# Sliding-window attention and two MLPs on one core: value products in quarter-array tiles, first query loads on ScalarE's queue, a new plan

## The chip, the cores and the metric

One NeuronCore of a Trainium2 chip runs the whole program. The metric is device time in microseconds, the median of several executions. Engines are named as in the profile: PE (TensorE, matmul), DVE (VectorE), ACT (ScalarE), POOL (GpSimd) and SP (SyncE, which issues DMAs).

## The reference

What is computed, cut to what matters:

```python
batch, n_heads, seq, head_dim = (2, 8, 768, 64)
n_sink, window = (4, 128)
scores = q @ k.T / sqrt(64); keep = is_sink | (0 <= row - col < window)
a = softmax(where(keep, scores, -1e9)); attn = a @ v
x = attn as (1536, 512)                  # tokens x model width
x = elu(x @ w_in) @ w_out                # 512 -> 2048 -> 512
x = (h - tanh(h)) @ w2_out, h = x @ w2_in
```

## The kernel before, in words

**Attention.** The 2 x 768 queries are 12 chunks `c` of 128 (six per batch). Each chunk has two groups `g` of four heads. A query needs the keys of its own chunk, of the one before (window 128) and the first eight keys (the sinks). `scores(g)` multiplies 64x64 tiles of the PE array, four at a time: the head width of 64 fills half the rows, and 64 queries fill half the columns. Each query half then has 128 keys in one "wide" piece, and a "thin" piece of 64 keys with 8 sink columns (72 columns). DVE adds the mask and takes the row's extreme in one instruction (a custom reduction, in the profile CUSTOM_DVE_ANT_0), ACT takes the exponential with its row sum, `norm(g)` divides, and `turn(g)` transposes the weights on PE into a PSUM bank, from which DVE or ACT copies them: `aT` (wide pieces), `aH` (thin pieces) and `aS` (sinks, split into a high and a low part).

**Value products.** `PV(c)` adds, for each of four head pairs, the sinks' product (all 128 columns), the wide pieces and the thin pieces into one bank of PSUM. The thin piece of a query half uses only 64 of the 128 key rows that stand in `aH`: the other 64 rows of its value tiles (`near_t`, `far_t`) are zeros, written once by eight memsets in `clear_values`, so each thin product streams through all 128 rows of the array, in a tile of 128x64 (two at once). Then `hi` and `lo` parts of the result are stored in `xhi` and `xlo`, the activations of the first MLP.

**MLPs.** Products are made in three float32r terms (high x high, high x low, low x high). `mlp_in` and `mlp_out` run over six phases of weight chunks; the first phase takes 256 tokens at a time (18 steps) and starts once two chunks of attention are done, all others take 512. Weights arrive as 64-bit words; `narrow` makes float32 of them (ACT, a clamp by `tensor_scalar`, then three DVE instructions), and `w_split` makes the two parts.

**What sets the order.** `Plan` records every instruction first, with the data it needs. `schedule` then simulates the engines with costs (`cost`), latencies between engines (`LAT`), a price for a change of the PE array's tiles (`SWITCH`), due times by kind of step (`DUE`), and the engines allowed for a kind (`PICK`), and fixes the order and the engine of every instruction. Where PE has nothing ready before the first `mlp_out`, it puts in idle matmuls (`idle`, a constant times a constant into bank 7), which keep PE busy: they are fixed instructions, executed whether or not the wait that they fill exists on the chip. All recorded instructions are issued from the line 404 (`emit` and the helpers), those of `many` (attention products) from line 165, idle matmuls from line 602.

The two lines that the change of the value products is about, for a thin piece (`last`):

```python
lhsT=part[:, kk, e, :] if last else whole[:, 2 * kk + e, :],
rhs=u[:, cols] if last else t[:, e, cols],
```

Of the kernel before, what the change touches and what calls it, by code (L numbers as in the profile page):

```python
# [7 lines left out]
F32 = mybir.dt.float32  # L8
# [8 lines left out]
P = 128  # L17
# [24 lines left out]
class Plan:  # L42
# [3 lines left out]
    ENGINES = ("PE", "ACT", "DVE", "POOL", "DMA")  # L46

    LAT = {
        "PE": {"PE": 0.0, "ACT": 205.0, "DVE": 210.0, "POOL": 235.0, "DMA": 200.0},
        "ACT": {"PE": 240.0, "ACT": 153.0, "DVE": 145.0, "POOL": 165.0, "DMA": 160.0},  # L50
        "DVE": {"PE": 262.0, "ACT": 130.0, "DVE": 127.0, "POOL": 160.0, "DMA": 130.0},
        "POOL": {"PE": 205.0, "ACT": 80.0, "DVE": 85.0, "POOL": 127.0, "DMA": 110.0},
        "DMA": {"PE": 2000.0, "ACT": 2000.0, "DVE": 2000.0, "POOL": 2000.0, "DMA": 0.0},
    }
# [3 lines left out]
    SWITCH = (95.0, 107.0, 55.0)  # L58
    BONUS, MARGIN = 159.46, 534669.58

    HOLD = {}
    DUE = {
        "c": (-4158.63, 122.021), "score": (-1557.88, 42.427), "norm": (-1579.49, 36.340), "end": (2474.55, 1.919),
# [7 lines left out]
        ("late w", "tensor_scalar", 512, False): ("DVE",), ("w", "tensor_scalar", 512, False): ("DVE",),  # L71
        ("T", "copy", 512, True): ("ACT",), ("norm", "tensor_scalar", 200, False): ("DVE",),
        ("late w", "copy", 512, False): ("ACT",), ("z", "copy", 512, False): ("ACT", "DVE"),
        ("ew", "tensor_tensor", 256, False): ("POOL",), ("late w", "tensor_tensor", 512, False): ("DVE",),
        ("late ew", "copy", 512, False): ("POOL",), ("out", "copy", 512, True): ("DVE",),
        ("late out", "copy", 512, True): ("DVE",), ("c", "tensor_copy", 128, False): ("POOL",),
        ("w", "copy", 512, False): ("ACT", "POOL"),
    }

    def __init__(self, tc):  # L80
# [7 lines left out]
        self.D = Rec(self, "DMA", nc.sync)  # L88

    def region(self, ap):  # L90
# [3 lines left out]
        if key not in self.masks:  # L94
            pstep, pn = dims[0]
            p0, e0 = divmod(off, pstep)
            psum = ap.space == PSUM
            grain = 512 if psum else (8 if pstep > 1024 else 1)
# [17 lines left out]
    def matmul_cost(kw):  # L116
# [5 lines left out]
        if kw["lhsT"].dtype == F32R:  # L122
            return n * 0.4233 + 10.3

        rows, cols = kw["lhsT"].shape[0] <= 64, kw["out"].shape[0] <= 64
        return (n / 1.2 + 2.5) * (0.5 if rows and cols else 1.0 if rows or cols else 2.0)

    @classmethod
    def cost(cls, eng, method, out, ins, kw):
# [6 lines left out]
        if eng == "ACT":  # L136
            t = (50.0 if psum else 100.0) + 0.833 * n
            return t + (94.0 if any(not isinstance(kw.get(k, 0.0), float) for k in ("scale", "bias")) else 0.0) \
                + (93.0 if "accum_out" in kw else 0.0) + (35.0 if "func" in kw else 0.0)
        if eng == "POOL":  # L140
            if method == "memset":
                return 60.0 + 0.5 * n
            return (60.0 + 3.6 * n if method == "tensor_scalar" else
                    60.0 + 1.8 * n if method == "tensor_copy" else 160.0 + 2.1 * n)
        if method in ("tensor_copy", "tensor_scalar", "memset") and not psum:
            return 75.0 + 0.525 * n
# [29 lines left out]
    def either(self, *recs, **kw):  # L176
# [7 lines left out]
        key = (self.tag[0], recs[1][1], cols, psum)  # L184
# [6 lines left out]
    def record(self, ways, args, kw, any_=False):  # L191
# [8 lines left out]
        for e, method, real in ways:  # L200
            if e == "DMA":
# [1042 lines left out]
```

## Time and profile before

| what | us |
|---|---|
| median of 3 runs (lowest, highest) | 626.07 (625.54, 627.9) |
| the profiled execution, its time | 626.38 |
| its span, first to last instruction | 624.6 |
| PE busy | 614.6 |
| DVE, ACT, POOL busy | 427.3, 239.8, 177.0 |

A busy PE is a PE whose instructions follow each other without a gap; their ends are modelled. What a piece of work costs PE is therefore read from start to start in the timeline, not from a row's mean. PE records a float32 product of attention as two matmuls, so 32 products are 64 records.

### The profile page before, as it was taken

To read this page: it belongs to the slowest core of one execution; us is meant where nothing else is said; L and a number is where in the kernel's file an instruction comes from. 1 tells how busy PE (TensorE), PEld (TensorE's weight loads), DVE (VectorE), ACT (ScalarE), POOL (GpSimd) and SP (SyncE) were. 2 spreads that over 40 slices of the span, in tenths; PEclk is the share of its full clock that TensorE was granted. 3 is DMA by queue.
4 is the path that set the end of the run, shared out by engine and by line. 5 is a ranking of instruction groups with operands and counts; after the bars stand their busy time and mean duration, and the time that the engine had idled before them with its cause. 6 is when DMAs were issued, how large, how long until landed. Compare 5 with 4: busy or idle time off the path is not lost.

```text
span 624.6 us, 11065 instructions
## 1 busy us (share of the span) xinstructions
PE 614.6 (98%) x4246; PEld 516.4 (83%) x4246; DVE 427.3 (68%) x955; ACT 239.8 (38%) x562; POOL 177.0 (28%) x225
## 2 busy tenths in 40 slices
PE   9999999999999999999999999999999999999995
PEld 6788889989888888888888888888888888888884
DVE  8889999999974779935379996368953543342232
ACT  6776978665413345332335441123411211111010
POOL 4335332403432333412121553223332121220120
PEclk9999999999999999999999999999999999999999
DMA  7577463443240122320012324022300000000012
GB/s 230 164 217 193 114 180 112 145 168 123 82 134 1 43 93 73 132 67 1 1 55 80 102 89 147 1 67 68 101 1 1 0 2 0 1 35 34 0 70 72
DMA packets 39038, 49.96 MB, mean 80 GB/s; under 512 B 25408, under 2 KB 26432, under 8 KB 38976
## 3 DMA queue, kind: packets, MB, share of 16 engines
q1 hardware_dynamic: 38976, 49.17, 25.1%
q8 instruction: 35, 0.57, 0.4%
q14 instruction: 27, 0.22, 0.1%
HBM read 46.01 MB, written 3.15 MB: 79 GB/s over the span
## 4 chain that ended last, share of the span: by engine, by line
PE 87%; DVE 6%; DMA 3%; ACT 2%; issue 1%; ACTq 0%; DVEq 0%
PE bank L404 78%; PE bank L165 8%; DVE arena L404 3%; DMA raw<-in_moe_w_in_dram 2%; DVE t L404 2%; PE bank L602 2%; ACT arena L404 1%; DVE w L404 1%; DMA arena<-in_kq_dram 1%; DMA small<-in_params_dram 0%; ACT t L404 0%; DVE xlo L404 0%; DVE xhi L404 0%; ACT arena_r L404 0%; DVE sm_all L404 0%
## 5 line engine op out<-in xcount | busy, mean ns | idle before, releaser
L404 PE MATMUL bank<-xhi,w 128*128 128x512 f32 (+1 forms) x840 | 246.5, 373 | 0.1
L404 POOL CAST arena_r<-arena 128x512 fp32r<-128x512 f32 (+2 forms) x115 | 80.2, 698 | 394.2 <-PE bank L404 234.4
L404 PEld LDWEIGHTS bank<-xhi,w 128*128 128x128 f32 x840 | 154.1, 188 | 27.8 <-DVE xhi L404 0.3
L404 PE MATMUL bank<-arena_r,w 128*128 128x512 f32 (+1 forms) x684 | 157.9, 358 | 0.7 <-DVE arena L404 0.6
L404 PE MATMUL bank<-w,arena_r 128*128 128x512 f32 (+1 forms) x594 | 154.3, 383 | 0.0
L404 PE MATMUL bank<-xlo,w 128*128 128x512 f32 (+1 forms) x420 | 143.8, 372 | 0.3 <-DVE xlo L404 0.3
L404 ACT ACTIVATE arena<-bank 128x512 f32<-128x512 f32 (+1 forms) x105 | 58.7, 559 | 221.5 <-PE bank L404 213.5
L404 PEld LDWEIGHTS bank<-arena_r,w 128*128 128x128 f32 x684 | 116.1, 189 | 20.5 <-DVE arena L404 1.6
L404 PEld LDWEIGHTS bank<-w,arena_r 128*128 128x128 f32 x594 | 109.4, 188 | 22.2
L404 DVE TENSOR_TENSOR arena_r<-arena,arena_r 128x512 fp32r<-128x512 f32 (+1 forms) x50 | 33.6, 673 | 85.4 <-PE bank L404 59.0
L404 PEld LDWEIGHTS bank<-xlo,w 128*128 128x128 f32 x420 | 78.9, 188 | 14.3 <-DVE xlo L404 0.5
L404 POOL TENSOR_TENSOR arena_r<-arena,arena_r 128x512 fp32r<-128x512 f32 (+3 forms) x77 | 79.1, 1029 | 25.8 <-ACT arena_r L404 6.9
L404 DVE TENSOR_TENSOR arena<-bank,arena 128x512 f32<-128x512 f32 (+1 forms) x65 | 43.1, 678 | 45.0 <-ACT arena L404 42.3
L404 ACT ACTIVATE arena<-arena 128x512 f32<-128x512 f32 (+1 forms) x73 | 42.3, 587 | 8.7 <-DVE w L404 6.1
L404 ACT ACTIVATE arena<-arena,nm_all 128x200 f32<-128x200 f32 (+1 forms) x96 | 42.2, 443 | 8.1 <-DVE nm_all L404 8.0
L165 PE MATMUL bank<-arena 128*64 128x64 f32 (+3 forms) x1376 | 43.5, 241 | 0.0
L165 PEld LDWEIGHTS bank<-arena 64*64 64x64 f32 (+1 forms) x1376 | 38.4, 135 | 4.8 <-issue 1.6
L404 DVE SCALAR_TENSOR_TENSOR arena<-arena,bank 128x512 f32<-128x512 f32 (+1 forms) x57 | 33.7, 595 | 12.6 <-ACT arena L404 12.6
L404 DVE TENSOR_SCALAR t<-t 128x512 f32<-128x512 f32 (+1 forms) x70 | 38.7, 559 | 1.6 <-ACT t L404 1.3
L404 DVE SCALAR_TENSOR_TENSOR t<-raw,t 128x512 uint32<-128x512 uint32 x54 | 39.7, 738 | 0.2
L404 DVE TENSOR_TENSOR w<-arena,w 128x512 fp32r<-128x512 f32 x29 | 25.7, 888 | 14.0 <-PE bank L404 7.3
L404 DVE TENSOR_SCALAR arena<-arena 128x512 f32<-128x512 f32 (+4 forms) x61 | 32.2, 530 | 1.9 <-ACT arena L404 1.0
(67 smaller groups left out, 459.6 us busy)
## 6 DMA issues: line engine op xcount, KB each, us to landing
raw<-in_moe_w_out_dram SPq DMA_DIRECT2D x20, 512.0 KB, 3.7
raw<-in_moe_w_in_dram SPq DMA_DIRECT2D x20, 512.0 KB, 4.0
arena<-in_moe_w_in_dram SPq DMA_DIRECT2D x12, 512.0 KB, 3.8
arena<-in_moe_w_out_dram SPq DMA_DIRECT2D x12, 512.0 KB, 3.8
arena<-in_kq_dram SPq DMA_DIRECT2D x22, 256.0 KB, 4.4
arena<-in_v_dram SPq DMA_DIRECT2D x12, 256.0 KB, 3.8
arena<-in_v_dram SPq DMA_DIRECT2D x40, 64.0 KB, 2.9
out_dram<-part SPq DMA_DIRECT2D x8, 256.0 KB, 2.2
```

What stands on the lines that cost most here:

```text
L165: eng.matmul(**kw)
L404: real(*self.ops[n][3], **self.ops[n][4])
L602: nc.tensor.matmul(out=bank[7][0:16, 0:256], lhsT=one[:, 0:16], rhs=one, start=True, stop=True)
```

## The change

- **Thin value products in 64x64 tiles.** The values of a chunk are loaded a second time with their halves of 64 rows swapped where needed (`r_vx`), so that each thin product has its 64 keys in either half of the array's rows. Zero padding, `near_t`, `far_t` and the memsets go. Wide products come first (16, in 128x64 tiles), then 16 thin ones in 64x64 tiles, four at once. The result `U` now takes half of two banks (2 and 3) in place of one whole bank. Heads are paired differently in `scores` to match.
- **Loads.** The first two chunks' queries are loaded by ACT's DMA queue (`E_`); chunk 0 comes in two pieces per tensor in place of three. The sinks' values come in eight strided loads.
- **Idle matmuls** fill all 128 output columns of the array in place of 16.
- **The plan**: new latencies and costs, new due times with an offset per step (`NUDGE`), and new engines: scalings of `norm` may go to POOL alone after the first six groups, the clamp of late weights goes to POOL, high parts of late hidden values to ACT.
- All eight banks become one PSUM tensor, `banks`.

The diff, cut to its core:

```diff
-        "ACT": {"PE": 240.0, "ACT": 153.0, "DVE": 145.0, "POOL": 165.0, "DMA": 160.0},
-        "DVE": {"PE": 262.0, "ACT": 130.0, "DVE": 127.0, "POOL": 160.0, "DMA": 130.0},
+        "ACT": {"PE": 200.0, "ACT": 153.0, "DVE": 145.0, "POOL": 165.0, "DMA": 160.0},
+        "DVE": {"PE": 140.0, "ACT": 115.0, "DVE": 127.0, "POOL": 180.0, "DMA": 130.0},
...
-    SWITCH = (95.0, 107.0, 55.0)
-    BONUS, MARGIN = 159.46, 534669.58
+    SWITCH = (95.0, 0.0, 55.0)
+    BONUS, MARGIN = 0.09, 15984.45
...
-        ("T", "copy", 512, True): ("ACT",), ("norm", "tensor_scalar", 200, False): ("DVE",),
+        ("norm", "tensor_scalar", 200, False): ("POOL",), ("norm", "tensor_scalar", 128, False): ("POOL",),
...
-        nc.tensor.matmul(out=bank[7][0:16, 0:256], lhsT=one[:, 0:16], rhs=one, start=True, stop=True)
+        nc.tensor.matmul(out=bank[7][:, 0:256], lhsT=one[:, 0:P], rhs=one, start=True, stop=True)
...
-            D_.dma_start(out=t[:, ps], in_=src[:, 1, ps])
+            (E_ if c < 2 else D_).dma_start(out=t[:, ps], in_=src[:, 1, ps])
...
-            for e, rows in enumerate(halves):
-                D_.dma_start(out=t[rows, :, e], in_=vt[of, keys].rearrange("p (a b) d -> p a b d", b=2)[:, :, e])
+        for need, rows, keys in ((i < NI - 1, top, bot), (i > 0, bot, top)):
+            if need:
+                D_.dma_start(out=x[rows], in_=vt[c, keys])
...
-        U = (b_tu0 if c < 3 else b_tu)(4, P)
+        U = banks[:, 2:4, 0:2 * P].rearrange("p a (h q) -> p a h q", h=2)
...
+        for half in range(2) if i else ():
             for m, cols in enumerate(halves):
+                for a in range(2):
                     for e, rows in enumerate(halves):
+                        side = halves[e ^ a]
+                        part.append(dict(
+                            out=U[rows, a, half, cols],
+                            lhsT=(v_t if m == e ^ a else vx_t)[c - m][side, 4 * a + 2 * half + e, :],
+                            rhs=aH_t[2 * c + half][side, a, cols], start=False, stop=True, skip_group_check=True,
```

What the plan makes of it, at three places. First PE, at the value products of chunk 1 and the scores beside them. In these rows `arena` holds queries, keys, values and weights of attention, `arena_r` sinks and hidden values; 64x64 rows are value products, 64x128 and 64x72 scores. Before:

```order
L165 MATMUL bank_83<-arena_r 128x128 x4
L165 MATMUL bank_83<-arena 64x64 x32
L165 MATMUL bank_80<-arena 64x128 x2
L165 MATMUL bank_81<-arena 64x128 x2
L165 MATMUL bank_80<-arena 64x72 x2
L165 MATMUL bank_81<-arena 64x72 x2
```

and now:

```order
L188 MATMUL banks<-arena_r 128x128 x4
L188 MATMUL banks<-arena 64x64 x16
L188 MATMUL banks<-arena 64x128 x4
L188 MATMUL banks<-arena 64x72 x4
L188 MATMUL banks<-arena 64x128 x4
L188 MATMUL banks<-arena 64x72 x4
L188 MATMUL banks<-arena 64x64 x16
```

The 32 products in half-array tiles became 16 wide ones and, behind the scores, which use 64x64 tiles already, 16 thin ones.

Second ACT, from its start to the first exponentials (`nm_all` holds the row extremes, `sm_all` the row sums). Before:

```order
L404 ACT_TABLE_LOAD
L404 ACTIVATE arena,sm_all<-arena,nm_all 128x128 x8
L404 ACTIVATE arena,sm_all<-arena,nm_all 128x200 x8
L404 COPY arena<-bank_83 128x512
L404 ACTIVATE arena,sm_all<-arena,nm_all 128x200 x4
```

and now, with buffer numbers:

```order
L428 DMA arena_78<-in_kq_dram 128x256 x2
L428 DMA arena_78<-in_kq_dram 128x512
L428 ACT_TABLE_LOAD
L428 ACTIVATE arena_78,sm_all_104<-arena_78,nm_all_103 128x128 x8
L428 ACTIVATE arena_78,sm_all_104<-arena_78,nm_all_103 128x200 x5
```

Three query loads stand ahead of the table load; SP's queue has the first key loads alone. On PE 14 idle matmuls stand ahead of the first scores where 32 stood; in the whole program there are 134 before and 134 now.

Third POOL, from the mask copies on, over the first chunks. Before:

```order
L404 MEMSET arena 64x4x64 x8
L404 COPY arena<-arena 64x128
L404 COPY arena<-arena 128x128
L404 COPY arena<-arena 128x80
L404 COPY arena<-arena 128x128
L404 TENSOR_SCALAR arena<-arena,sm_all 128x128 x3
L404 CAST arena_r<-arena 128x64
L404 TENSOR_TENSOR arena_r<-arena,arena_r 128x32
```

and now:

```order
L428 COPY arena<-arena 128x80
L428 TENSOR_SCALAR arena<-arena,sm_all 128x128 x3
L428 TENSOR_SCALAR arena<-arena,sm_all 128x200 x4
L428 TENSOR_TENSOR arena_r<-arena,arena_r 128x4x8
L428 TENSOR_SCALAR arena<-arena,sm_all 128x200 x2
L428 TENSOR_TENSOR arena_r<-arena,arena_r 128x4x8 x2
L428 CAST arena_r<-arena 96x512
L428 TENSOR_SCALAR arena<-arena,sm_all 128x200 x5
```

Of the 80 scalings of 200 columns DVE keeps 9 (it had all 80), POOL takes 71, and the 58 clamps of 512 columns for late weights move from DVE to POOL as well.

## Rows read from the trace of the kernel before

**Rows 1.** The page: busy time, and two engines' busy tenths in 40 slices

```profile
PE 614.6 (98%) x4246; PEld 516.4 (83%) x4246; DVE 427.3 (68%) x955; ACT 239.8 (38%) x562; POOL 177.0 (28%) x225
...
PE   9999999999999999999999999999999999999995
...
DVE  8889999999974779935379996368953543342232
```

**Rows 2.** Waits of PE: us in total, times, longest us

```profile
PE bank L165 <- ACT arena_r L404: 1.5, 2, 1.0
PE bank L602 <- PEq L1198: 0.8, 1, 0.8
PE bank L404 <- DVE arena L404: 0.6, 1, 0.6
PE bank L404 <- DVE xlo L404: 0.3, 1, 0.3
```

**Rows 3.** Windows: stretch, length, busy (x instructions), clock, DMA share, GB/s

```profile
10.00:20.00 10.00, 10.00 (x182) 7.32 (x175) 9.69 (x53) 7.98 (x31) 2.28 (x7) 1.00 0.92 293
...
450.00:500.00 50.00, 50.00 (x222) 41.41 (x221) 25.39 (x42) 9.05 (x15) 10.83 (x11) 1.00 0.00 1
```

**Rows 4.** Timeline of PE, the start: start us, us, then the instruction

```profile
0.77 5.37 PE L602 MATMUL bank<-const-bfloat16-1.0 128*16 128x256 bf16 x32 [0.77 <-PEq L1198]
6.07 0.67 PE L165 MATMUL bank<-arena 64*64 64x128 f32 x16
6.67 0.72 PE L602 MATMUL bank<-const-bfloat16-1.0 128*16 128x256 bf16 x5
...
12.26 0.92 PE L165 MATMUL bank<-arena 64*64 64x128 f32 x32
13.11 0.66 PE L165 MATMUL bank<-ident,arena 128*128 128x128 f32 x4
```

**Rows 5.** Timeline of PE: value products, entered at 46.39, whole at 114.00

```profile
46.13 0.33 PE L404 MATMUL bank<-arena_r,w 128*128 128x256 f32 x1
46.39 0.33 PE L165 MATMUL bank<-arena 128*64 128x64 f32 x3
...
114.00 2.08 PE L165 MATMUL bank<-arena 128*64 128x64 f32 x64
116.02 0.66 PE L165 MATMUL bank<-ident,arena 128*128 128x128 f32 x4
```

**Rows 6.** Timeline of PE: idle matmuls and transposes in turn

```profile
20.34 1.05 PE L602 MATMUL bank<-const-bfloat16-1.0 128*16 128x256 bf16 x8
21.33 0.44 PE L165 MATMUL bank<-ident,arena 128*128 128x128 f32 x2
...
21.80 1.61 PE L602 MATMUL bank<-const-bfloat16-1.0 128*16 128x256 bf16 x13
23.34 0.87 PE L165 MATMUL bank<-ident,arena 128*128 128x128 f32 x6
...
24.26 0.72 PE L602 MATMUL bank<-const-bfloat16-1.0 128*16 128x256 bf16 x5
```

**Rows 7.** DMA issues up to 12 us: count, KB each, median us to landing

```profile
arena<-in_kq_dram SPq DMA_DIRECT2D x2, 128.0 KB, 2.8
```

**Rows 8.** Timeline of DVE, as rows 4: reductions, scalings, the store of xlo

```profile
6.77 0.29 DVE L404 CUSTOM_DVE_ANT_0 arena<-bank,arena 128x128 f32<-128x128 f32 x1
...
13.13 1.02 DVE L404 TENSOR_SCALAR arena<-arena,sm_all 128x200 f32<-128x200 f32 x4
...
30.23 2.24 DVE L404 TENSOR_SCALAR arena<-arena,sm_all 128x200 f32<-128x200 f32 x4
...
33.05 0.69 DVE L404 TENSOR_TENSOR xlo<-bank,xhi 128x512 fp32r<-128x512 f32 x1 [0.30 <-ACT xhi L404]
```

**Rows 9.** Groups by shape, first 125 us: xcount | busy us, mean ns

```profile
L404 DVE CUSTOM_DVE_ANT_0 arena<-bank,arena 128x200 f32<-128x200 f32 x80 | 25.1, 355 | 1.1 <-PE bank L165 0.9
L404 POOL TENSOR_SCALAR arena<-arena,sm_all 128x128 f32<-128x128 f32 x7 | 4.6, 663 | 7.0 <-DVE sm_all L404 7.0
```

More of the change, by code (lines that the diff above doesn't have):

```diff
@@ L68 @@
+    DUE = {
+        "c": (-3598.10, 112.400), "score": (-1546.08, 68.951), "norm": (-1516.12, 67.772), "end": (2602.63, 50.065),
[4 rows of a table added]
     }
     PICK = {
[L71 to L74 removed]
@@ new lines @@
+        ("first T", "copy", 128, True): ("ACT",), ("first T", "copy", 64, False): ("ACT",),
+        ("ew", "copy", 256, False): ("ACT",), ("T", "copy", 64, False): ("ACT", "POOL"),
+        ("w", "copy", 512, False): ("ACT", "POOL"), ("late w", "tensor_scalar", 512, False): ("POOL",),
+        ("z", "copy", 512, False): ("DVE", "POOL"), ("ew", "tensor_tensor", 256, False): ("DVE",),
+        ("late ew", "copy", 512, False): ("ACT",), ("out", "copy", 512, True): ("DVE",),
+        ("late out", "copy", 512, True): ("DVE",), ("first T", "tensor_tensor", 32, False): ("POOL",),
@@ L78 @@
+        ("first T", "copy", 512, True): ("ACT",),
     }
@@ L204, in record @@
                     size *= k
-                costs[e] = (max(600.0, 0.0111 * size * outs[0].shape[0]), real, 0)
+                costs[e] = (max(480.0, 0.0111 * size * outs[0].shape[0]), real, 0)
             else:
@@ L487, in tile_sink_attention__two_mlps @@
              F32R: arena_p.tile([P, 2464], F32R, name="arena_r")}
-    bank = [banks_p.tile([P, 512], F32, name=f"bank{n}") for n in range(8)]
+    banks = banks_p.tile([P, 8, 512], F32, name="banks")
+    bank = [banks[:, n] for n in range(8)]
     top_of = {}
@@ L741, in scores @@
                         K = (own if i == 0 or m != part else prev)[rows, p]
-                        to = S[e][cols, pr, slice(*(wide, thin)[part][pr])]
+                        f = pr ^ e
+                        to = S[e][cols, f, slice(*(wide, thin)[part][f])]
                         if part == 0:
@@ L823, in PV @@
                 for kk in range(4)
             ])
-        mm = []
+        full, part = [], []
         for kk in range(4):
-            g, pr = 2 * c + kk % 2, kk // 2
-            t = aT_t[g][:, pr]
-            if i == 0:
+            a, half = divmod(kk, 2)
+            g = 2 * c + half
+            for m, cols in enumerate(halves if i else (slice(0, P),)):
                 for e, rows in enumerate(halves):
-                    mm.append(dict(
-                        out=U[rows, kk], lhsT=v_t[c][:, 2 * kk + e, :], rhs=t[:, e],
-                        start=True, stop=True, skip_group_check=True,
-                    ))
-                continue
-            u = aH_t[g][:, pr]
+                    full.append(dict(
+                        out=U[rows, a, half, cols], lhsT=v_t[c - 1 if i and m == 0 else c][:, 2 * kk + e, :],
+                        rhs=aT_t[g][:, a, e ^ a, cols], start=not i, stop=not i, skip_group_check=True,
+                    ))
@@ L837, in PV @@
+        for half in range(2) if i else ():
             for m, cols in enumerate(halves):
-                whole, part = (v_t[c - 1], near_t[c]) if m == 0 else (v_t[c], far_t[c])
-                for last in range(2):
+                for a in range(2):
                     for e, rows in enumerate(halves):
-                        mm.append(dict(
-                            out=U[rows, kk, cols],
-                            lhsT=part[:, kk, e, :] if last else whole[:, 2 * kk + e, :],
-                            rhs=u[:, cols] if last else t[:, e, cols],
-                            start=False, stop=bool(last), skip_group_check=True,
-                        ))
@@ L856, in attention @@
         build_early()
-        clear_values()
         load_params()
```

103 lines of the change are left out of this document (59 added, 44 removed), and 11 rows, old and new, of tables (DUE, NUDGE).

## The prediction

> **What bounds the kernel now.** Read the page first: PE is busy 98% of the span, in every slice but the last [rows 1], so work taken from PE's stream can shorten the run, and nothing else can unless it removes one of PE's waits. The waits of PE come second: the list has 3.2 us, of which 0.8 is the start [rows 2]. Read third how full the other engines are: in the slices of attention DVE is nearly as full as PE, 9.7 of 10 us from 10 to 20 [rows 1, 3], while from 450 to 500 us PE does 222 matmuls in 50 us, 0.225 us each, and DVE idles half the time [rows 3]. So the MLP stretch is matmul-bound and its products don't change; what can move lies in the first 120 us, where PE carries attention, MLP products and 134 idle matmuls, and DVE stands close behind it. "Busy" there holds idle matmuls too: at the start 32 of them run before the first scores [rows 4]. They are fixed instructions, so PE's stream is a sum of starts, whatever it waits for.
>
> **The change, part by part.** All of it is a sum against the profiled execution, 626.4 us (span 624.6 and 1.8 around it), which is 0.3 above the median of the runs.
>
> *Thin value products.* For a chunk, 32 products take 114.00 to 116.02, 2.02 us [rows 5]; less some 0.1 for leaving the tile shape, that is 0.060 us each. 16 of them become products of 64 columns in 64x64 tiles. The nearest price is the thin score piece, 72 columns in the same tiles: eight wide and eight thin scores take 0.85 us (12.26 to 13.11), eight wide ones 0.60 (6.07 to 6.67), so eight thin ones take 0.25, 0.031 each [rows 4]. A saving of 16 x 0.029 = 0.46 per chunk, in ten of twelve chunks (each batch's first has no thin piece): **-4.6**. The ends: 0 if they don't run four at once, -5.1 if the price goes with the columns (64/72 of 0.031). I take the row as it stands.
>
> The rule that speaks against it is that of the Trainium skill, "TensorE: Matmul & The Clock Gate", section "Wait — 56ns, not 53.3ns?": starts of matmuls never come closer than about 25 ns, however small. With two records per product, 16 products would then take 16 x 2 x 25 ns = 0.80 us, the saving would be 1.6 and the time 623.3. This trace differs: 16 records of 72 columns take 0.25 us, 16 ns each [rows 4]. As a mechanism it is rival C.
>
> *Idle matmuls at full width.* Between transposes, eight idle matmuls take 0.99 (20.34 to 21.33) and thirteen 1.54 (21.80 to 23.34): 0.11 each, and 0.11 once for what follows. Three transposes take 0.47 (21.33 to 21.80), seven 0.92 (23.34 to 24.26): 0.112 each, and 0.13 once [rows 6]. So going from 16 columns to 128 or back costs about 0.12, like any change of tile. The order of before has 21 places where an idle matmul stands next to a full-width one: 21 x 0.12, **-2.5**. The ends are -2.5 and 0 (if the cost is that of idle matmuls and not of their width). An idle matmul streams 256 columns at either width, and both programs have 134 of them: 0.
>
> *Other changes of tile.* The listing has 60 before and 64 now. Entering the value products costs 0.26 (46.13 to 46.39) where half of a 512-column product is 0.11 [rows 5, 3]: 4 x 0.15, **+0.6**. In seven of ten chunks the thin products stand behind scores that need 64x64 tiles anyway, so the split adds a change in three chunks only.
>
> *Start and loads.* 32 idle matmuls take 5.30 us, 0.166 each against 0.11 later [rows 4, 6]: the first ones run slow. Now 14 stand there, so PE asks for the first scores after 14 x 0.11 to 14 x 0.22, 2.3 to 3.9 us into the span. A key load of 128 KB takes 2.8 us from issue to landing [rows 7]; no queue starts before PE does, at 0.77 [rows 4], and the keys stand behind the parameters, so they can hardly be there before 4. The wait that takes the idle matmuls' place is 0 to 1.7 us; I take 0.5, since the slow price is that of the first idle matmuls. Fewer slow idle matmuls give back 0.3. Together **+0.2**. The idle matmuls that left the head stand later (28 follow the first scores). The query loads on ACT are hidden: ACT has nothing to do before the first reduction, at 6.77 [rows 8]. What is queued behind them is the table load, ahead of the first exponential. The memsets and half of the value loads' issues go at no cost or gain on PE: neither POOL nor SP ends a wait in rows 2.
>
> *What moves between engines.* DVE gives up 71 scalings of 0.255 us (13.13, four in 1.02) [rows 8], 18 us of its fullest stretch; POOL takes them. The one place where DVE may still end last is the way to the first MLP product, which needs the second chunk's xlo, now at 33.05 [rows 8]. By the listing DVE has between its first reduction and that store 28 reductions (at most 0.31 each, 8.7) [rows 9], 14 scalings (3.6), three stores of x (0.69 each, 2.1) [rows 8], eight instructions on weights and some 25 small ones (together about 7.5, an estimate at 0.6 and 0.1): 22 us, so 28.5 if it starts at 6.5. PE's own stream gets there at about 28 (that store ends at 33.7 now; less the 2.5 of the idle matmuls, one chunk's 0.5, and 2.5 of scores, transposes and tile changes that the plan now puts behind it). They arrive together, so I charge **+0.5** for a wait there. With it the new plan is tight: it expects DVE's results on PE after 140 ns where it expected 262. Waits of the size in rows 2 may go or come back elsewhere; I leave them as they are, and let 3 us either way into the range.
>
> Sum: 626.4 - 4.6 - 2.5 + 0.6 + 0.2 + 0.5 = 620.6, and by the median 0.3 less: **620.3 us**.
>
> **The rivals.**
>
> *A: the front belongs to DVE.* POOL, busy with scalings, slows DVE. For it: four scalings took 2.24 us at 30.23 where four took 1.02 at 13.13 [rows 8]. Had the 14 scalings left to DVE in the front 0.56 each, the first MLP product would come 14 x 0.305 = 4.3 us later, PE would stand in waits in place of idle matmuls, and the time would be 624.6. Against it: in the slow place POOL ran work with two inputs, in the front it will run scalings with one, and most of DVE's front is reductions, which read PSUM. The Trainium skill says so too ("GPSIMD Engine Reference", section "Key points"): GpSimd shares its SBUF interfaces with VectorE, and they contend when VectorE reads through two ports. By that rule the slow price would hold whenever POOL works; the trace shows it in one place. Chance 0.17.
>
> *B: POOL becomes the bound, slower than before.* POOL's price for 128 columns is 0.66 us [rows 9]. For 200 columns it lies between 0.66 and 1.04 (in proportion), for a 512-column clamp between 0.66 and 2.65. Up to the end of attention, some 107 us, POOL has 71 + 11 scalings, eight clamps and a dozen others: at the upper ends 74 + 7 + 21 + 8 = 110 us, more than there is; at 0.9 and 2.0, where a fixed part would put them, 64 + 7 + 16 + 8 = 95, which fits. It decides from about 100 on, since POOL waits for data too. Then attention stretches by some 12 us past what PE can fill, as late weights pass through the same engine: 632. Against it: POOL is busy for 177 of 625 us now, 2.3 of 10 from 10 to 20 [rows 1, 3], and the plan has MLP products to put in between. Chance 0.07.
>
> *C: starts, not the array, pace the thin products.* 64 records of value products start 0.032 us apart now (2.02 / 64) [rows 5]. If thin ones do the same, since they are shorter than scores and add to banks that other tiles write, nothing is saved there: 624.9. The scores' tiles share banks as well, and start 0.016 apart [rows 4]. Chance 0.04. The page on TensorE named above would put it at 623.3.
>
> *D: the waits go too.* Scalings leave DVE, loads are fewer, latencies fit better: most of the 2.4 us of waits behind the start [rows 2], and the 0.5 charged above, vanish: 617.5. Chance 0.10.
>
> **How the numbers follow.** The forecast has 0.62, and by itself 618 to 623. A measurement of this kernel can tell 0.5%, 3.1 us, from no change, so faster means below 622.9: nearly all of the forecast, all of D, a little of A: 0.73. Between 622.9 and 629.2 lie the rest of the forecast, most of A, and C: 0.19. Slower is B and mishaps that I don't see: 0.08. The range reaches over A and C at the top and to one us under D at the bottom: 616.5 to 625.5. It leaves out B, and the ends of D and A, some 2 in 10.
>
> **What would show it.** In the profile of the changed kernel: a chunk's wide and thin products together at 1.5 us without the scores between them (2.02 now); an idle matmul between transposes that costs 0.11 and nothing once; the first scores at 4 to 4.5 us in place of 6.07; the second chunk's xlo stored by 28 to 30 us in place of 33.7; PE's waits at 3 to 5 us in sum. Rival A would show as waits of PE on xlo or on transposes' inputs between 10 and 35 us and scalings on DVE at over 0.4 us; B as POOL at 9 tenths up to 120 us and PE waiting for POOL or for weights; C as thin products at 0.9 us for 16. The forecast is wrong if PE's stream has become shorter as said and its waits have grown by as much.

## The result, and the profile after

The changed kernel takes 629.75 us (median of 20 runs, 627.68 to 635.55), the kernel before 626.16 on the same chip: 1.0060 times its time, 95% interval 1.0044 to 1.0076. It is slower by 3.8 us; the forecast was 620.3, its range ended at 625.5. The profiled execution took 628.59 us (span 626.8); that of before 626.38. Over the 20 executions of the changed kernel the time tends to go with the clock: the four slowest (631.4 to 635.6 us) have a mean granted clock of 0.987 to 0.994, the four fastest (627.7 to 628.5) one of 0.994 to 0.998.

The page of the changed kernel answers to [rows 1]: PE is as full as before in most slices, DVE is emptier, POOL fuller, and the granted clock has a notch in its sixth slice. PE's busy time fell by 1.3 us only (614.6 to 613.3), where the forecast took 6.8 from its stream (-4.6, -2.5, +0.6, and 0.3 of slow idle matmuls); the span outside it grew by 3.5, from 10.0 to 13.5.

```profile
PE 613.3 (98%) x4246; PEld 517.3 (83%) x4246; DVE 391.4 (62%) x851; ACT 292.5 (47%) x665; POOL 279.2 (45%) x218
...
PE   8999989999999999999999999999999999999995
...
PEclk9999989999999999999999999999999999999999
```

Waits of PE, against [rows 2]: they make 6.6 us (3.2 there), most of it behind ACT and a load.

```profile
PE banks L188 <- ACT arena_r L428: 2.0, 2, 1.7
PE banks L188 <- ACT arena L428: 1.6, 3, 0.8
PE banks L188 <- DMA arena<-in_kq_dram: 1.3, 2, 1.0
PE banks L188 <- POOL arena_r L428: 0.9, 2, 0.6
PE banks L627 <- PEq L1219: 0.8, 1, 0.8
```

Timeline of PE at the start, against [rows 4]. Fourteen idle matmuls end, PE waits for the keys, and the second chunk's scores start at 11.59 us (8.95 in the trace of before).

```profile
0.76 3.15 PE L627 MATMUL banks<-const-bfloat16-1.0 128*128 128x256 bf16 x14 [0.76 <-PEq L1219]
4.95 1.13 PE L188 MATMUL banks<-arena 64*64 64x128 f32 x16 [1.04 <-DMA arena<-in_kq_dram]
6.29 1.13 PE L188 MATMUL banks<-arena 64*64 64x128 f32 x16 [0.21 <-DMA arena<-in_kq_dram]
7.35 4.31 PE L627 MATMUL banks<-const-bfloat16-1.0 128*128 128x256 bf16 x28
11.59 1.60 PE L188 MATMUL banks<-arena 64*64 64x128 f32 x64
```

The 28 idle matmuls take 4.24 us, 0.15 each, where later ones take 0.11; sixteen scores take 1.13, where before they took 0.67. So PE still runs slow here, by its pace alone: the column of the granted clock has 1.00 in this stretch.

Timeline of PE, value products apart, and transposes next to idle matmuls, against [rows 5, 6]:

```profile
19.93 0.66 PE L188 MATMUL banks<-ident,arena 128*128 128x128 f32 x4
20.42 0.72 PE L627 MATMUL banks<-const-bfloat16-1.0 128*128 128x256 bf16 x5
20.98 0.82 PE L188 MATMUL banks<-ident,arena 128*128 128x128 f32 x6
...
119.50 0.33 PE L428 MATMUL banks<-xlo,w 128*128 128x256 f32 x1
119.76 1.15 PE L188 MATMUL banks<-arena 128*64 128x64 f32 x32
120.84 0.38 PE L428 MATMUL banks<-xhi,w 128*128 128x256 f32 x1
121.16 0.69 PE L188 MATMUL banks<-arena 64*64 64x64 f32 x32
121.78 0.38 PE L428 MATMUL banks<-xhi,w 128*128 128x256 f32 x1
```

Wide products take 1.08 us, thin ones 0.62, each with the way out of its tile; together 1.70, where it was 2.02 with one way out and the forecast said 1.5. In a chunk whose two parts stand apart, then, 0.32 us is saved. Five idle matmuls take 0.56, 0.11 each and nothing once, as forecast.

Timeline of DVE, against [rows 8], its first reduction and the second chunk's xlo, and the window that answers to the first of [rows 3]: DVE starts sooner and is busy 6.33 of 10 us (9.69 before), POOL 4.79 (2.28), and xlo is 0.75 us later all the same.

```profile
6.10 0.29 DVE L428 CUSTOM_DVE_ANT_0 arena<-banks,arena 128x128 f32<-128x128 f32 x1 [0.28 <-PE banks L188]
...
33.80 0.68 DVE L428 TENSOR_TENSOR xlo<-banks,xhi 128x512 fp32r<-128x512 f32 x1
```

```profile
10.00:20.00 10.00, 10.00 (x218) 8.35 (x217) 6.33 (x38) 6.61 (x27) 4.79 (x7) 1.00 1.04 269
```

The largest single loss in the trace is at 85 us. First SP in the trace of before, at the first batch's sink values, then three timelines of the changed kernel (SP, ACT, PE), and the windows behind (length, busy of PE, PEld, DVE, ACT, POOL, clock, DMA share, GB/s):

```profile
20.12 3.38 SPq L404 DMA_DIRECT2D arena<-in_v_first_dram  x7
```

```profile
76.47 6.10 SPq L428 DMA_DIRECT2D arena<-in_v_first_dram  x8
82.69 0.35 SPq L428 DMA_DIRECT2D raw<-in_moe_w_in_dram  x1
```

```profile
86.55 0.66 ACT L428 ACTIVATE t<-raw 128x512 f32<-128x512 f32 x1 [2.54 <-DMA raw<-in_moe_w_in_dram]
87.11 0.25 ACT L428 CAST arena_r<-banks 96x128 fp32r<-96x128 f32 x1
```

```profile
85.11 0.61 PE L428 MATMUL banks<-arena_r,w 128*128 128x256 f32 x3
87.42 0.44 PE L188 MATMUL banks<-ident,arena 128*128 128x128 f32 x2 [1.70 <-ACT arena_r L428]
```

```profile
86.00:88.00 2.00, 0.56 (x3) 0.33 (x3) 0.52 (x4) 1.45 (x6) 2.00 (x4) 1.00 0.73 209
88.00:90.00 2.00, 2.00 (x34) 1.66 (x35) 1.94 (x5) 2.00 (x8) 2.00 (x2) 0.50 0.00 0
90.00:92.00 2.00, 2.00 (x17) 1.87 (x19) 2.00 (x13) 1.95 (x10) 1.56 (x2) 0.65 0.82 172
```

SP spends 6.1 us on the eight strided loads of the second batch's sink values. The raw weights behind them are issued at 82.69; ACT, which takes its work in order, stands 2.54 us before them, and behind that instruction stand the copies that empty the transposes' banks. PE stands still for some 2 us, and then the granted clock is at 0.50, the lower of its two levels (1.2 GHz), up to some 91.4 us (by the 0.65 of the next window): 32 scores take 1.54 us there (88.20 to 89.74), 0.85 in [rows 4]. Half clock for 3.4 us costs some 1.7, an estimate from the two levels.

### The profile page after: what moved, and what is told of

It reads as the page before. It is cut to its first block, busy times and chain, and to the rows that moved or that the text cites. A ratio compares the mean times of both kernels' runs of the same rounds, so it can differ in the third digit from the quotient of the medians.

```text
span 626.8 us, 11017 instructions
## 1 busy us (share of the span) xinstructions
PE 613.3 (98%) x4246; PEld 517.3 (83%) x4246; DVE 391.4 (62%) x851; ACT 292.5 (47%) x665; POOL 279.2 (45%) x218
## 4 chain that ended last, share of the span: by engine, by line
PE 89%; DMA 4%; ACT 3%; DVE 3%; SPq 1%; issue 0%; DVEq 0%; ACTq 0%
PE banks L428 82%; PE banks L188 6%; ACT arena L428 2%; DMA raw<-in_moe_w_in_dram 2%; DVE arena L428 1%; DMA raw<-in_moe_w_out_dram 1%; DMA arena<-in_kq_dram 1%; PE banks L627 1%; SPq L428 1%; DVE t L428 0%; DVE w L428 0%; DVE arena_r L428 0%; ACT t L428 0%; ACT arena_r L428 0%; DVE sm_all L428 0%
## 5 line engine op out<-in xcount | busy, mean ns | idle before, releaser
L428 PE MATMUL banks<-xhi,w 128*128 128x512 f32 (+1 forms) x840 | 251.6, 374 | 0.0
L428 PEld LDWEIGHTS banks<-xhi,w 128*128 128x128 f32 x840 | 154.4, 188 | 27.7 <-DVE arena L428 0.2
L428 PE MATMUL banks<-arena_r,w 128*128 128x512 f32 (+1 forms) x684 | 159.4, 358 | 0.1
L428 PE MATMUL banks<-w,arena_r 128*128 128x512 f32 (+1 forms) x594 | 154.6, 383 | 0.1
L428 PE MATMUL banks<-xlo,w 128*128 128x512 f32 (+1 forms) x420 | 147.7, 373 | 0.0
L428 PEld LDWEIGHTS banks<-arena_r,w 128*128 128x128 f32 x684 | 116.6, 188 | 19.8 <-DVE arena_r L428 0.3
L428 PEld LDWEIGHTS banks<-w,arena_r 128*128 128x128 f32 x594 | 109.4, 188 | 22.7 <-DVE arena L428 0.4
L428 ACT CAST arena_r<-arena 128x512 fp32r<-128x512 f32 (+2 forms) x121 | 66.3, 548 | 128.2 <-PE banks L428 122.7
L428 PEld LDWEIGHTS banks<-xlo,w 128*128 128x128 f32 x420 | 79.1, 189 | 13.5
L428 POOL TENSOR_SCALAR arena<-arena,sm_all 128x200 f32<-128x200 f32 (+1 forms) x82 | 72.6, 900 | 18.8 <-ACT arena L428 7.5
```

The lines of the kernel that those rows point to most:

```text
L428: real(*self.ops[n][3], **self.ops[n][4])
```

## The experiments

The ratio is to executions of the kernel before on the same chip, and what an edit is worth is read from ratios; 0.001 of the ratio is 0.63 us. The last column is where the first MLP product starts in the profile (33.6 in the kernel before).

| run | us | ratio (95% interval) | first product |
|---|---|---|---|
| the change | 629.75 | 1.0060 (1.0044 to 1.0076) | 33.5 |
| e1_head | 631.32 | 1.0072 (1.0051 to 1.0093) | 34.1 |
| e2_sinks | 626.02 | 0.9991 (0.9978 to 1.0004) | 34.4 |
| e3_both | 625.11 | 0.9975 (0.9962 to 0.9987) | 33.5 |
| e4_idle | 624.70 | 0.9975 (0.9963 to 0.9988) | 33.5 |
| e5_acts | 624.48 | 0.9982 (0.9970 to 0.9994) | 31.3 |
| e6_dve | 631.34 | 1.0091 (1.0073 to 1.0109) | 32.6 |
| e7_fill | 631.10 | 1.0105 (1.0067 to 1.0142) | 33.2 |
| e8_before_sinks | 625.88 | 0.9987 (0.9975 to 0.9999) | 34.8 |
| e9_oldplan | 626.95 | 1.0012 (1.0003 to 1.0022) | 35.0 |
| e10_lat | 622.18 | 0.9943 (0.9930 to 0.9957) | 30.9 |
| e11_fill | 628.49 | 1.0053 (1.0039 to 1.0067) | 33.2 |
| e12_before_lat | 626.43 | 0.9997 (0.9985 to 1.0008) | 36.2 |
| e13_lat_eight | 625.21 | 0.9983 (0.9971 to 0.9995) | 32.2 |
| e14_lat2800 | 628.46 | 1.0025 (1.0011 to 1.0039) | 34.0 |
| e15_lat4300 | 623.58 | 0.9964 (0.9947 to 0.9981) | 30.8 |
| e16_one | 627.64 | 1.0021 (1.0003 to 1.0040) | 33.2 |
| e17_twice | 626.80 | 1.0003 (0.9992 to 1.0015) | 32.3 |
| e18_narrow_idle | 624.73 | 0.9964 (0.9951 to 0.9977) | 31.8 |

### The start, the sink loads, and both

```diff
 e1: emit, after schedule()
+ moved = first 6 idle matmuls behind PE's first real instruction
+ self.order = moved + the rest
 e2: load_v, layout
- 8 strided loads r[to:96:4, ...] <- vs, per batch
+ one load r[0:96] <- vs[b]; layout() orders the rows
 e3: both
```

> Six of the 28 idle matmuls that follow the first scores stand ahead of them (20 there, 22 behind); nothing else differs from the changed kernel. Theory (the start was paid in clock): with no hole in PE's stream the granted clock rises at about 4.3 us into the span (9.5 in the changed kernel), the second chunk's first scores start at about 9 (11.6), the first MLP product comes some 2 us sooner (33.6), and the time falls by 2 to 2.5 us, to about 627.4. Rival (the front belongs to the chain through DVE, ACT and POOL): the clock rises early and the scores come early, but the first MLP product stays at 33.2 to 33.6 and the time at 629 to 630.

> The first keys' values of a batch lie in memory in the order in which the kernel wants them, and come with one load per batch in place of eight; all other instructions and their order are those of the changed kernel. Theory (SP's queue): the raw weight load behind them is issued some 5 us sooner (82.7 in the changed kernel), ACT no longer stands 2.5 us in its wait for it, PE's stall of 2 us at 85 and the half clock from 88.0 to 91.4 vanish: 3 to 4 us less, about 626. Rival: the raw load waits for its buffer or for earlier readers, not for SP's turn; then PE's stall stays within 0.5 us of what it is, and so does the time, 629 to 630.

> Both edits together. Theory: two stretches of half clock go, 5 to 6 us less than the changed kernel, about 624, below the kernel before by some 2 us; and the runs of the kernel lie closer together than those of the changed kernel. Rival for the head alone (its gain is taken back by the first MLP product's inputs): about 626, the same as with one load per batch alone. Rival for both: 629 to 630.

**The start alone gave nothing** (1.0072 against 1.0060). The timeline of PE in e1_head:

```profile
6.78 2.64 PE L631 MATMUL banks<-const-bfloat16-1.0 128*128 128x256 bf16 x22
9.35 1.60 PE L188 MATMUL banks<-arena 64*64 64x128 f32 x64
...
23.39 0.44 PE L188 MATMUL banks<-ident,arena 128*128 128x128 f32 x2 [1.10 <-ACT arena L432]
24.47 0.31 PE L188 MATMUL banks<-ident,arena_r 128*96 128x128 f32 x1 [0.63 <-POOL arena_r L432]
...
34.07 0.36 PE L432 MATMUL banks<-xhi,w 128*128 128x256 f32 x1
```

The idle matmuls run at 0.12 each and the scores come 2.2 us sooner, but the transposes at 23 wait longer (0.25 us before the first of them in the changed kernel), and the first MLP product is no sooner. That is what the rival said of the front. In this execution (633.14 us) the granted clock is at 0.50 for 3.4 us behind these waits, from 25.4, and for 6.8 us behind a stall of 2.93 us at 89.5. Its executions with a mean clock of 0.996 or more (629.68 and 629.80 us) are no faster than the changed kernel's with such a clock either (627.7 to 629.6).

**One sink load gave 4.3 us** (0.0069 of the ratio), a little more than the theory's 3 to 4. Timelines of SP, ACT and PE in e2_sinks:

```profile
77.92 0.57 SPq L431 DMA_DIRECT2D arena<-in_v_first_dram  x1
78.60 0.37 SPq L433 DMA_DIRECT2D raw<-in_moe_w_in_dram  x1
```

```profile
85.10 0.69 ACT L433 ACTIVATE t<-raw 128x512 f32<-128x512 f32 x1
```

```profile
86.30 0.61 PE L433 MATMUL banks<-arena_r,w 128*128 128x256 f32 x3
86.75 0.38 PE L189 MATMUL banks<-ident,arena 128*128 128x128 f32 x2
```

The raw weights are issued 4.1 us sooner, ACT does not wait, PE goes on after 0.45 us where it took 2.31, and the clock stays. Between the two profiled executions the gain is 2.2 us (628.59 and 626.35): 1.9 of stall and 1.7 of half clock, less the 1.2 by which e2 comes to this place later. The rest of the 4.3 is a difference between executions of which no trace was kept. Both edits gave 1.0 us more than the load alone, less than the 2 expected, and the two intervals overlap.

### The idle matmuls' width, and the sink load in the kernel before

```diff
 e4: before.py, idle()
- out=bank[7][0:16, 0:256], lhsT=one[:, 0:16]
+ out=bank[7][:, 0:256], lhsT=one[:, 0:P]
 e8: before.py, load_v and layout
- 7 loads r <- vs, per batch
+ one load r[0:96] <- vs[b]
```

> The kernel before with full-width idle matmuls (128 columns in place of 16) and nothing else: its plan and every order stay. Prediction's term by itself: 21 changes of tile at 0.12 us less on PE, 2.5 us, about 623.7. Rival (the front is paced by the chain through DVE, so PE only waits where it idled before): less than 0.7 us, 625.5 to 626.3. In both cases the idle matmuls between transposes cost 0.11 each and nothing once.

> The kernel before with one load of the first keys' values per batch in place of seven, in the order in which it wants them; all else as it was. Theory (its seven loads, 3.4 us of SP's time per batch, stood on no path, so one load per batch mends only what the changed kernel's eight strided loads broke): 625.8 to 626.8, no difference. Rival (one load would have helped the kernel before as well, and the comparison with one load is no fair one): 1 to 3 us less, 623.5 to 625.5.

Width alone gave 1.6 us (0.8 to 2.3), between theory and rival. The first product is hardly sooner (33.47), so what the front saved went into waits (0.71 us for keys at 16.5, 0.49 for POOL at 28.8) and the gain lies behind it. One load helped the kernel before by 0.8 us, at the edge of what can be told (0.1 to 1.6): most of the 4.3 mends what the eight strided loads broke.

### ACT's order, and the scalings' engine

```diff
 e5: e3, the order's times of 9 instructions on raw weights
+ ("w", 0): ACT at 20.8, DVE at 22.6; ("w", 1): ACT at 22.3, DVE at 24.6
+ ("w", 2): ACT at 31.8, DVE at 31.9 to 32.4
 e6: the change, emit
+ every "norm" scaling from group 6 on: DVE's instruction in POOL's place
```

> The kernel with both edits, and nine instructions on the first three weight halves stand later in the order of ACT and DVE: ACT's first reading of the raw weights behind the copies and exponentials of attention that it now blocks, DVE's clamps behind them. Theory (ACT and DVE take their work in order, and stand before raw weights that have not landed): in the kernel with both edits ACT waits 2.7, 1.6 and 2.2 us for raw weights at 17.5, 21 and 34.5 us, DVE 2.3 us behind the first, and PE idles or waits meanwhile; now the transposes at 22.5 come 2 us sooner, the first MLP product at 30.5 to 32 (33.5), and the time falls by 1.5 to 3 us, to 622 to 623.5. Rival (the weights themselves, or the loads behind which they come, set the first MLP product): it stays at 33.2 to 33.8, the time at 624.6 to 625.6.

> The changed kernel, in whose order the 72 scalings from the fourth chunk on run on DVE in place of POOL; nothing else. Theory (the prediction's: DVE is the fuller engine, and giving up 18 us there is worth it): DVE stands 18 to 23 us longer in the first 125 us, PE waits for its reductions more often, 2 to 5 us slower, 632 to 635. Rival (POOL's 0.9 us per scaling makes the transposes late, so the move to POOL was a part of the loss): PE's waits shrink, 627 to 629.

The timeline of ACT in e3_both, which e5 set out from, shows the two waits:

```profile
20.24 0.69 ACT L437 ACTIVATE t<-raw 128x512 f32<-128x512 f32 x1 [2.70 <-DMA raw<-in_moe_w_in_dram]
22.55 0.66 ACT L437 ACTIVATE t<-raw 128x512 f32<-128x512 f32 x1 [1.63 <-DMA raw<-in_moe_w_out_dram]
```

With them out of attention's way the first product came 2.1 us sooner, as expected. The ratio did not follow (0.9982 against 0.9975), though in the profiled execution PE's waits fell from 6.9 to 5.1 us; this repair by hand is not shown to be worth anything, and why not stays open. Scalings back on DVE cost 1.9 us, with intervals that just overlap, in an order made for POOL: nothing here says that their move to POOL was a part of the loss.

### Is the stall paid in clock too?

```diff
 e7, e11: the change, emit
+ 16 idle matmuls ahead of the second transposes of group 17 (e7), 15 (e11)
```

> The changed kernel with 16 more idle matmuls ahead of the transposes before which PE stands still for 2 us at 85.4 us; the late load and ACT's wait stay. Theory (the stall is paid twice, once as a wait and once in clock): the wait shrinks to what the idle matmuls leave of it, PE goes on as late as before, at about 87.4, but the granted clock stays at its upper level behind it, and 1.5 to 1.8 us come back: about 628. Rival 1 (the clock is not lost by the stall): 629.5 to 630. Rival 2 (PE was held by something that the idle matmuls now delay): 631 to 632.

> The changed kernel with 16 more idle matmuls at the place of its long stall itself, ahead of the transposes of group 15 (the run with 16 of them ahead of group 17 had them at 99 us, where PE did not wait, and shows their price there, 1.8 us of PE's stream). Theory (the stall is paid twice, as a wait and in some executions in clock): the idle matmuls take up 1.3 to 1.8 us of the wait, PE goes on no later than before, at about 87.4, no execution shows a granted clock under 0.99, and the median falls by 0.5 to 1.5 us, to 628.2 to 629.2. Rival (what follows the stall is not held up by the clock): 629.5 to 630.5. Second rival (the wait is shorter than the idle matmuls in most executions): 631 or more.

e7 missed its place. e11 stood at the right one, but did not fill the wait: its idle matmuls write into the bank that ACT had yet to empty, and waited themselves. Timeline and window of PE in e11_fill:

```profile
87.60 1.95 PE L630 MATMUL banks<-const-bfloat16-1.0 128*128 128x256 bf16 x16 [1.74 <-ACT arena_r L431]
89.39 0.38 PE L188 MATMUL banks<-ident,arena 128*128 128x128 f32 x2
```

```profile
88.00:90.00 2.00, 2.00 (x25) 1.00 0.09 26
```

The transposes come 2 us later than in the changed kernel, the clock stays at its upper level, and the time is the same within the intervals. So neither run tests the theory. In the profile of e7 the same stall stands up to 89.02 us (1.82 us behind ACT's copy), and the clock stays at 1.00 behind it. The other profiles say more. e1 and e6 have the stall as well, of 2.93 and 1.32 us, and half clock behind both. A window of PE in e1_head, whose mean clock of 0.66 is 6.8 us at 0.50:

```profile
90.00:100.00 10.00, 9.98 (x157) 0.66 0.37 110
```

In three of the five profiles with this stall (the change, e1 and e6, not e7 and e11) half clock follows it, for 3.4 to 6.8 us; in the other fifteen the column shows no half clock up to 600 us. So the stall is paid in clock too, in some executions. What decides in which stays open.

### Whose plan, and what it believes of loads

```diff
 e9: the change with one sink load
- LAT, SWITCH, DUE, NUDGE, PICK, cost() and ACT's loads of the change
+ those of before.py, all loads on SP
 e16: the change with one sink load in the plan too, planned anew
 e14, e10, e15: e16, and in LAT
- "DMA": 2000.0 to every engine
+ "DMA": 2800.0 (e14), 3500.0 (e10), 4300.0 (e15)
 e13: e10 with the eight strided loads kept
 e12: before.py with 3500.0
```

> The changed kernel's code (narrow value products, their operands and loads, full-width idle matmuls) with one load of the first keys' values per batch, planned with the kernel before's tables and costs, all loads on SP. Theory (the code gains, the new order loses): the head starts with about 30 idle matmuls as before, scalings stay on DVE, ACT does not stand over 2 us before a raw weight at 85; what the pieces have measured so far (thin products 3.4 less over PE's stream, idle matmuls 1.9 less) arrives, 620.5 to 623. Rival (waits of this size come with the narrow products, since PE is done sooner and stands before the same chains, whatever the plan): 624 to 627.

> The changed kernel with one load of the first keys' values per batch, planned anew with one constant changed: a load's data counts as there 3.5 us after its issue is through, in place of 2.0. Theory (the plan puts ACT's and PE's instructions ahead of loads that have not landed, because its loads land too soon): more idle matmuls ahead of the first scores, no wait of ACT over 1 us for a raw weight between 15 and 90 us, 621.5 to 624. Rival (due times and nudges belong to the old constant, a new order makes other waits of the same size): 625 to 629.

> The kernel before, planned anew with the one constant: a load's data counts as there 3.5 us after its issue is through, in place of 2.0. Theory (the constant matters where the rest of the plan is tight, and the kernel before, whose latencies to PE are larger and whose scalings are on DVE, has little to gain): 625 to 628. Rival (the constant alone is worth 4 us to any of these kernels, so the gain of the replanned kernel has nothing to do with the change): 621 to 623.5.

> The changed kernel with its eight strided loads per batch, planned anew with 3.5 us in place of 2.0. Theory (the constant was the cause, the eight loads only one of the places where it bit): most of the gain stays, 622.5 to 625. Rival (SP's 6 us per batch are a cost of their own, which no order hides): 626 to 629.

> As the kernel planned with 3.5 us and one load per batch, with 4.3 us. Theory (the constant should be at least what loads take; their medians are 4.0 to 5.0 us from issue to landing, of which the plan counts 0.5 to 1.5 as the issue's own time): about as good, 621.5 to 624. Rival (the order at 3.5 us was a lucky one among many): 625 to 628.

> The changed kernel with one load of the first keys' values per batch, planned anew with its own constant of 2.0 us: the control for the two kernels planned with 3.5 and 4.3 us. Theory: as the kernel in which the eight loads were replaced and the order kept, 625.5 to 627.5; the first scores stand behind 14 idle matmuls and wait for their keys, ACT waits for raw weights. Rival (planning anew with one load in place of eight gives the gain, not the constant): 621.5 to 623.5.

> As the kernels planned anew with one load per batch and 2.0, 3.5 and 4.3 us (627.6, 622.2 and 623.6 us), with 2.8 us. Theory (the time falls as the constant comes up to what loads take): between the neighbours, 623.5 to 626.5. Rival (orders scatter by some 2 us whatever the constant, and these three fell as they did by chance): at or above 627.6, or below 622.

**The theory of e9 fell**: with the old tables, too, the new code brings no gain. So the missing gain isn't due to the new tables alone. The planner put 17 more idle matmuls into that order (PE has 4263 records, 4246 before), some 1.9 us at 0.11 each, and PE is as busy as before (615.0 us, 614.6 there): a part of what the products gave up was filled up again.

**e10 beats both kernels**, by 3.6 us against the one before. Timeline of PE in e10_lat:

```profile
0.76 5.37 PE L627 MATMUL banks<-const-bfloat16-1.0 128*128 128x256 bf16 x28 [0.76 <-PEq L1214]
6.06 1.10 PE L188 MATMUL banks<-arena 64*64 64x128 f32 x32
...
30.89 0.37 PE L428 MATMUL banks<-xhi,w 128*128 128x256 f32 x1
```

The planner, told that loads land later, puts 28 idle matmuls at the head by itself; the first scores wait for nothing, and the first product is 2.7 us sooner than in both kernels. But the waits that the theory meant did not go. PE's waits make 6.3 us (6.6 in the changed kernel), and ACT still stands before a raw weight, longer than in e3:

```profile
22.05 0.67 ACT L428 ACTIVATE t<-raw 128x512 f32<-128x512 f32 x1 [3.13 <-DMA raw<-in_moe_w_out_dram]
```

What fell most is PE's busy time, 609.8 us for 613.3: there is no half clock at 88 us, and the second chunk's scores start at 10.34 in place of 11.59. So the constant, or the order that it made, helped in another way than was expected. Planning anew without the constant (e16) is 4.9 us slower than with it, and the constant does nothing for the kernel before (e12). With the eight loads the time is 2.5 us longer even in an order made with them (e13 against e10). But the time does not fall step by step: 2.8 us is as slow as 2.0, as the rival of e14 (orders scatter) had it. Four orders at four constants, two fast, two slow, don't settle how much of the 4.9 is the constant and how much the luck of one order; two orders of the same code with one load and 2.0 us (e2, e16) lie 1.9 us apart. The fast two have their first product at 30.8 to 30.9, the slow two at 33.2 and 34.0.

### The prediction's two terms, in the good order

```diff
 e17: e10, emit
+ each group of 16 thin value products issued twice
 e18: e10, idle()
+ 16 columns, as in before.py
```

> The kernel planned with 3.5 us, in which every group of 16 thin value products is issued twice in a row (the thin part of the values is counted twice in the output). Theory (in this order PE's stream sets the time, and a thin product costs what the trace shows): 10 groups by 16 products at 0.031 us, as the prediction had them, 5.0 us more, 627.2; at 0.016, the pace of four at once, 2.6 more, 624.8. Rival (attention's stretch waits for other engines, and PE's own work hides in it): under 1 us more, 622.2 to 623.2.

> The kernel planned with 3.5 us, with idle matmuls of 16 columns as the kernel before has them; all else as it was. Its trace has 15 places where an idle matmul stands next to a full-width one. Theory (such a change of tile costs 0.10 to 0.12 us, as in the kernel before, where full width gave 1.85 us for 18 such places in its trace): 1.5 to 1.8 us more, 623.7 to 624. Rival (the idle matmuls stand where PE would wait anyway): under 0.5 us more, 622.2 to 622.7.

The same value products in the timeline of PE, e10_lat first (one group's scores, 32 records, come last in both), then e17_twice:

```profile
27.42 2.47 PE L188 MATMUL banks<-arena 128*64 128x64 f32 x96
29.81 0.66 PE L188 MATMUL banks<-ident,arena 128*128 128x128 f32 x4
```

```profile
28.34 2.93 PE L188 MATMUL banks<-arena 128*64 128x64 f32 x128
31.21 0.66 PE L188 MATMUL banks<-ident,arena 128*128 128x128 f32 x4
```

2.39 against 2.87 us: 16 thin products cost 0.48, 0.030 each. By ten groups that is 4.8; the time rose by 3.8 (0.0060 of the ratio; the two intervals allow some 2.7 to 4.9, so that 4.8 fits and the 2.6 of the lower price hardly does). Idle matmuls of 16 columns cost 1.3 us there (0.0021), though the two intervals still overlap a little.

## Why the prediction was wrong

- **Thin products, -4.6: the price was right.** 0.030 each was measured for the 0.031 taken from the scores. That the saving reaches the time is shown only in the order of e10, by doubling them; with the old tables (e9) it did not. Thirty-two records start within 0.62 us, 0.019 apart with the way out in it, which ends rival C. The floor of about 25 ns that the Trainium skill states ("TensorE: Matmul & The Clock Gate", section "Wait — 56ns, not 53.3ns?") isn't seen here, between records of four tiles at work at once.
- **Idle matmuls, -2.5: right in kind, too large.** It was 1.6 us in the kernel before. An idle matmul at full width costs 0.11 and nothing once, as forecast; but such places stand where PE waits, and part of what is saved there becomes a longer wait.
- **Other changes of tile, +0.6**: no run prices it alone, and the 0.32 us saved in a chunk whose parts stand apart says that the way in and out of a second tile counts. 0.26 us into the value products (119.50 to 119.76) is the price that was taken.
- **Start and loads, +0.2: wrong.** The keys' wait came out as bounded (1.04 and 0.21). (SP's first issue is at 0.73 us, not behind PE's start at 0.77 as the forecast had it; nothing hangs on it.) What was not charged is that PE goes on slowly behind it: the second chunk's scores are 2.6 us late. Yet it is not where most of the time was lost: the first product comes when it came before, and e1, whose scores come sooner, is no faster.
- **"The memsets and half of the value loads' issues go at no cost or gain on PE: neither POOL nor SP ends a wait in rows 2." This is the step that failed.** SP had ended no wait before, but the change gives it eight strided loads per batch, 0.76 us of issue each, where seven took 3.38 us in the trace of before (20.12 us). They were mentioned in the change and priced nowhere. What stands behind them on SP is a weight load, behind it ACT, and behind ACT PE. By e2 this is 4.3 of the 9.5 us between the forecast and the result, and with one load in their place the change is as fast as the kernel before (0.9991). The other 5.2 no run takes apart; the trace of the changed kernel says where a part of it lies.
- **"PE's stream is a sum of starts, whatever it waits for": this failed as well.** The profiled execution, with the loss at 85 us in it, is 8.0 us above its forecast of 620.6. Of these, 5.5 are PE's busy time, which fell by 1.3 and not by 6.8, and 2.5 the span outside it, which grew by 3.5 and not by 1.0. The forecast's own sign of being wrong, a stream shorter as said with waits that grew as much, is not what came. A price per start holds at one pace: the half clock at 88 us took some 1.7, and the slow pace of the head some 3.7 (14 and 28 idle matmuls against 0.11 each, twice 16 records of scores against 0.037), where in the kernel before it took some 1.7 and the forecast gave 0.3 back. These are estimates from the rows shown; they leave about 1.5 open.
- **"Waits of the size in rows 2 may go or come back elsewhere; I leave them as they are": wrong too.** They doubled, from 3.2 to 6.6. Between 17 and 23 us ACT stands before raw weights for 4.3 us in e3; the load issued at 15.08 there lands after 7.5 us, with keys and values on their way as well, where the plan counts 3.45 (1.45 for the issue, 2.0 behind it). The Trainium skill ("DMA: Bandwidth & Descriptors", section "Anatomy of one DMA — SWDGE (gpsimd) path") gives 2.0 us plus the bytes at 436 GB/s for one transfer on that path, an estimate of 3.2 us for these 512 KB. Loads here go by SP, and the traces have 3.9 us (82.69 to 86.55) to 7.5. The forecast read the plan's new latencies as "tight" for DVE and did not ask which loads its order takes for landed.
- **Rival A, DVE: not it.** DVE begins its first reduction sooner, and its nine scalings take 0.36 us each in the timeline (0.26 before, 0.56 by the rival), about 1 us in all. Its store of xlo, due at 28 to 30 by the forecast, comes at 33.80; with ACT's readings of raw weights moved back (e5) it comes at 31.78, 33.72 without (e3). **Rival B, POOL: no.** A scaling of 200 columns takes 0.93 us on POOL (0.9 was taken), and with them back on DVE the kernel isn't faster. The side was B's, the mechanism was not. The chance of slower, 0.08, was all "mishaps that I don't see": the one that came could be seen in the diff.

With the sink load made one and the plan told of later loads, the same code takes 622.18 us, inside the range of 616.5 to 625.5. That does not make the forecast right: of four constants two give such a time, and it comes without the fall in waits.

## What to carry to other kernels

When a change rewrites loads, price each issue on the queue that makes it, and follow that queue: the next load, the engine that first reads it, and what stands behind that instruction on its engine. A hand-made planner is as good as its belief in when loads land; put the measured landing, under traffic, beside the constant, and try more than one order before believing a gain. A price per start is a price at one pace: ask where the change makes PE stand still, and what pace it goes on at. If the front ends when it did although PE's work in it became less (first MLP product at 33.47 us in e4, 33.59 before), PE alone does not set its end.

## What the runs showed of the hardware

- A load of 24 rows with a stride of four partitions costs SP 0.76 to 0.81 us of issue (6.10 and 6.50 for eight, 24 KB each); one load of 96 rows with all their 192 KB costs 0.57 to 0.85 (e2, e3).
- A stall of PE of 1.3 to 2.9 us at 85 to 89 us was followed by a granted clock of 0.50 for 3.4 to 6.8 us in three profiles (the change, e1, e6) and by none in two (e7, e11). The changed kernel's 20 executions spread over 7.9 us, the 12 of e2, in which the stall is gone, over 4.0.
- POOL takes 0.93 us for a scaling of 200 columns, and 2.06 for a clamp of 512:

```profile
L428 POOL TENSOR_SCALAR arena<-arena,sm_all 128x200 f32<-128x200 f32 x71 | 65.2, 933 | 11.3 <-DVE sm_all L428 7.0 <-ACT arena L428 3.2 <-ACT w L428 0.8
L428 POOL TENSOR_SCALAR t<-t 128x512 f32<-128x512 f32 x7 | 14.4, 2058 | 0.0
```
